# Batch 2's scores two steps earlier, its token cast ahead of batch 1's exponentials, and the states of batches 2 and 3 fetched sooner

## The chip, the cores and the metric

The kernel runs on one core of one Trainium2 chip. A core has five engines with a queue of instructions each: TensorE (PE in the profile; its weight loads are PEld), VectorE (DVE), ScalarE (ACT), GpSimd (POOL) and SyncE (SP), which here only issues DMAs. Each engine runs its queue in order and waits at an instruction until the semaphores that it names have been raised. The metric is the device time of one execution in microseconds; a time is the median of several runs.

## The reference

Eight batches of 512 tokens and 32 states, eight heads of 64 numbers each, go through a cross attention in both directions, and what comes out goes through a feed-forward layer with a leaky ReLU:

```
scores  = scale * x @ state^T          # tokens look at states
a       = softmax(scores);   xread = a @ state
scores2 = scale * state @ x^T          # states look at tokens
a2      = softmax(scores2);  sread = a2 @ x
x       = concat([xread, sread])       # 4352 rows of 512
out     = leaky_relu(x @ w_in, 0.01) @ w_out      # w_in 512x2048, w_out 2048x512
```

## The kernel before, in words

The product xread @ w_in is never made from xread. For each batch the states are multiplied with w_in first (`a_m`, line 339: the result M has 256 rows, one for each head and state, and 2048 columns, made in four column chunks of 512), and the hidden layer is then M^T times the softmax weights aT (`ff1`, line 369: two matmuls of 128x512 for each of 16 steps, and a ScalarE Prelu out of PSUM, line 377; `ff1_pair`, line 379, does two steps into one bank pair). `piece` (line 481) is four matmuls of the second layer for a block of 128 tokens; after the last of its four quarters the block is copied out of PSUM (`y_store`, line 494) and stored by a DMA from SP.

A batch goes through these stages before its `ff1`:

- `load_x` (line 97): the tokens come as fp32 into `xl`, of which there is one buffer, so that the next batch's load waits for the casts out of it. Batch 2's load is issued on GpSimd's queue early on, behind the loads of the weights and of batch 1's tokens (`x1`).
- `cast_x` (line 104): tokens to bf16, in halves on ScalarE and GpSimd for batch 2 and on GpSimd alone later.
- `a_xt_dma` (line 189): a transposing DMA from SP makes `xT`.
- `load_state` (line 166) fetches the states of two batches (first group: 2 and 3) with eight small DMAs from SP, after a VectorE memset of the same tile; `state_t` (line 175) casts them on GpSimd and transposes them by a DMA from SP (`st_t`).
- `a_scores` (line 202): eight matmuls into the PSUM tile `sc`. There is one such tile for all batches.
- `a_shift`, `a_exp`, `a_probs`: the softmax over states (VectorE, one ScalarE exponential at line 233, VectorE), which gives aT. `a_max2`, `a_exp2` (two exponentials straight out of `sc`, line 274), `a_probs2`: the softmax over tokens, which gives a2, and `a_a2t`, its transposing DMA from SP.

The order of all instructions is written by hand: each engine runs its own in the order in which the program's text issues them. PSUM is shared by tags: "ph" and "py" have two banks each and "big" and "sc" are one pair of banks each. So `a_m(a2, 0, "big")` and the wide `ff1_pair` of steps 6 and 10, also "big", must take turns, and an eviction (`m_evict`, line 359) ends each turn.

The stretch that the change touches begins at line 835, where batch 0's hidden layer is done and batch 1's tokens are cast (VectorE, line 836). Batch 0's second layer fills TensorE while batch 1 is prepared: its tokens are transposed on TensorE (line 853), then come its scores, its M and its softmax. Lines 869 to 888 hold batch 1's second exponentials, the states' and tokens' preparation of batch 2 and the load of batch 3. The loop at line 895 then does the 16 steps of batch 1's hidden layer. After each odd step a `piece` is slipped in (two last ones of batch 0, then six of batch 1), after step 5 batch 2's scores and its first chunk of M, at step 7 the transposing DMA of batch 3's tokens, and at steps 9, 11 and 13 batch 2's exponentials. Lines 916 to 921 close the stretch: both batches' `a_probs2`, batch 1's `a_a2t`, and two more chunks of M. From line 927 on, batches 2 to 7 run through a steady loop whose second layer is done by a scheme with fewer multiplications (line 557).

Of the kernel before, what the change touches and what calls it, by code (L numbers as in the profile page):

```python
# [10 lines left out]
B, H, S, D = 8, 8, 512, 64  # L11
# [16 lines left out]
def kernel(  # L28
# [9 lines left out]
    nc = tc.nc  # L38
# [15 lines left out]
    VEC, SCA, POO = nc.vector.tensor_copy, nc.scalar.copy, nc.gpsimd.tensor_copy  # L54
# [49 lines left out]
    def cast_x(b, h0, h1, copy):  # L104
        copy(  # L105
            xs[b][:, :, h0:h1].rearrange("p t h d -> p h t d"),
            xl[b][:, h0:h1].rearrange("p h (t d) -> p h t d", t=NT),
        )
# [54 lines left out]
    stf = [consts.tile([P, hi - lo, P], FP32, name=f"stf{lo}", tag=f"stf{lo}") for lo, hi in groups]  # L163
    stb = [consts.tile([P, hi - lo, P], BF16, name=f"stb{lo}") for lo, hi in groups]

    def load_state(i):
        lo, hi = groups[i]
        for k in range(NK):
            for g in range(2):
                nc.sync.dma_start(  # L170
                    stf[i][NS * k:NS * (k + 1), :, D * g:D * (g + 1)],
                    state[lo:hi, 2 * k + g].rearrange("b n d -> n b d"),
                )
# [10 lines left out]
    def a_open(a, b):  # L184
        a.b = b
        a.xb = xs[b]
        a.xT = att.tile([P, NT, NK, P], BF16, name="xT", tag="xT")
# [43 lines left out]
    def block_exp(sh, n):  # L231
        e1 = att.tile([P, n * NS], BF16, name="e1", tag="e1", bufs=1)
        nc.scalar.activation(out=e1[:], in_=sh[:], func=AF.Exp, scale=SCALE)
        return e1

    def block_probs(dst, e1, n):
        r1 = att.tile([P, n], FP32, name="r1", tag="r1")
        nc.vector.tensor_reduce(
            out=r1[:], in_=e1[:].rearrange("p (c j) -> p c j", j=NS),
            axis=AX.X, op=ALU.add, apply_transpose=True,  # L240
        )
        nc.vector.tensor_scalar(out=r1[:], in0=r1[:], scalar1=1e-9, scalar2=None, op0=ALU.add)
        q1h = att.tile([P, n], BF16, name="qh", tag="qh")
        with nc.allow_low_precision(reason="one rounding, of the finished reciprocal"):
            nc.vector.reciprocal(q1h[:], r1[:])
        q1b = att.tile([P, n, NS], BF16, name="qb", tag="qb", bufs=1)
        nc.vector.transpose(q1b[:], q1h[:, :, None].to_broadcast([P, n, NS]))
        nc.vector.tensor_tensor(
            out=dst, in0=e1[:].rearrange("p (g s) -> p g s", g=2),
            in1=q1b[:].rearrange("p (g c) j -> p g (c j)", g=2), op=ALU.mult,  # L250
        )
# [5 lines left out]
    def a_exp(a):  # L257
        a.e1 = block_exp(a.sh, NB)

    def a_probs(a):  # L260
        a.aT = att.tile([P, 2, S], BF16, name="aT", tag="aT")
        block_probs(a.aT[:], a.e1, NB)

    def a_max2(a):
        m2 = att.tile([P, 2], FP32, name="mcol", tag="mcol")
        nc.vector.tensor_reduce(out=m2[:], in_=a.sc[:], axis=AX.X, op=ALU.max, negate=True)  # L266
        a.m2s = att.tile([P, 2], FP32, name="mcols", tag="mcols")
        nc.vector.tensor_scalar(out=a.m2s[:], in0=m2[:], scalar1=SCALE, scalar2=None, op0=ALU.mult)

    def a_exp2(a, g):  # L270
        if g == 0:
            a.e2 = att.tile([P, 2, S], BF16, name="e2", tag="e2")
            a.r2 = att.tile([P, 2], FP32, name="r2", tag="r2")
        nc.scalar.activation(  # L274
            out=a.e2[:, g], in_=a.sc[:, g, :], func=AF.Exp,
            bias=a.m2s[:, g:g + 1], scale=SCALE, accum_out=a.r2[:, g:g + 1],
        )

    def a_probs2(a):
        nc.vector.tensor_scalar(out=a.r2[:], in0=a.r2[:], scalar1=1e-9, scalar2=None, op0=ALU.add)  # L280
        q2 = att.tile([P, 2], FP32, name="qc", tag="qc")
        nc.vector.reciprocal(q2[:], a.r2[:])
        a.a2 = att.tile([P, 2, S], BF16, name="a2", tag="a2")
        for g in range(2):
            nc.vector.tensor_scalar(
                out=a.a2[:, g, :], in0=a.e2[:, g, :],
                scalar1=q2[:, g:g + 1], scalar2=None, op0=ALU.mult,
            )

    def a_a2t(a):  # L290
        a.a2T = att.tile([P, 2, NT, P], BF16, name="a2T", tag="a2T")
        nc.sync.dma_start_transpose(
            a.a2T[:].rearrange("p g i q -> p (g i) q"), a.a2[:].rearrange("p g s -> p (g s)")
        )
# [64 lines left out]
    def m_evict(a, c, pm, copy):  # L359
        cols = slice(DM * c, DM * (c + 1))  # L360
        if isinstance(pm, list):
            for g in range(2):
                copy(a.M[:, g, cols], pm[g][:])
        else:
            copy(a.M[:, :, cols], pm[:])  # L365
# [115 lines left out]
    def piece(b, hT, i, jq, bank=None, copy=SCA):  # L481
        if jq == 0:
            y = ys[b, i] = Y()
            y.py = psum.tile([P, DM], FP32, name="py", tag="py")[:] if bank is None else bank
        y = ys[b, i]
        for j in range(4 * jq, 4 * jq + 4):
            nc.tensor.matmul(  # L487
                y.py, lhsT=hT[:, j, P * i:P * (i + 1)], rhs=w_out_bf[:, j, :],
                start=(j == 0), stop=(j == 15),
            )  # L490
        if jq == 3 and copy is not None:
            y_store(b, i, copy)

    def y_store(b, i, copy):
        tag, bufs = (f"yo{i - 2}", 1) if (b, i) in ((0, 2), (0, 3)) else ("ysb", 3)
        ysb = ypool.tile([P, DM], FP32, name="ysb", tag=tag, bufs=bufs)
        copy(ysb[:], ys[b, i].py)
        if b == B:
            for bb in range(4):
                r0 = (4 * i + bb) * SROW + S  # L500
                nc.sync.dma_start(out[r0:r0 + NS, :], ysb[NS * bb:NS * (bb + 1), :])
        else:
            nc.sync.dma_start(rows_of(b)[i], ysb[:])
# [140 lines left out]
    a0, a1, a2 = att_of[:3]  # L644
# [149 lines left out]
    def open_ff1_0(tag):  # L794
        if tag == "sc":
            pr = psum.tile([P, 2, S], FP32, name="php", tag=tag, bufs=1)
            return pr, [pr[:, 0], pr[:, 1]]
        ph = [psum.tile([P, S], FP32, name="ph", tag=tag) for _ in range(2)]
        return ph, [p[:] for p in ph]

    def ff1_0(banks, j, g, vs=(0, 1)):
        for v in vs:
            nc.tensor.matmul(  # L803
                banks[v], lhsT=a0.M[:, g, P * (j + v):P * (j + v + 1)], rhs=a0.aT[:, g, :],
                start=(g == 0), stop=(g == 1),
            )
# [19 lines left out]
    for j, tag in ((4, "py"), (6, "sc"), (8, "py"), (10, "ph"), (12, "py"), (14, "ph")):  # L826
        t, bk = open_ff1_0(tag)
        for g in range(2):
            ff1_0(bk, j, g)
        relu0(t, j)  # L830
        if j == 8:
            m_evict(a0, 3, a_m(a0, 3, "big"), VEC)
            a_scores(a0)
            a_max2(a0)
    for u in range(2):
        VEC(
            a1.xb[:, :, NK * u:NK * (u + 1)].rearrange("p t h d -> p h t d"),
            x1[u][:].rearrange("p h (t d) -> p h t d", t=NT),
        )
    nc.vector.memset(stf[0][:, 0, D - 1:D + 1], 0.0)  # L840
    load_state(0)

    for g in range(2):
        a_exp2(a0, g)
# [21 lines left out]
    for i in (2, 3):  # L866
        piece(0, h0, i, 1)
    m_evict(a1, 3, a_m(a1, 3, "ph"), SCA)
    for g in range(2):
        a_exp2(a1, g)  # L870
    open_xb(2)
    state_t(0)
    cast_x(2, 0, 4, SCA)
    cast_x(2, 4, 8, POO)
    a_open(a2, 2)
    a_xt_dma(a2)
# [17 lines left out]
    fill = [(0, h0, 0, 3), (0, h0, 1, 3)] + [(1, h1, i, jq) for jq in range(3) for i in range(2)]  # L894
    for s in range(16):
        if s in (6, 10):
            ff1_pair(a1, h1, s, "big")
        elif s not in (7, 11):
            ff1(a1, h1, s)
        if s == 5:  # L900
            a_scores(a2)
            m_evict(a2, 0, a_m(a2, 0, "big"), SCA)
            a_shift(a2)
            a_max2(a2)
        if s % 2:
            pb, hT, i, jq = fill[s // 2]
            piece(pb, hT, i, jq, copy=VEC if s == 3 else SCA)
        if s == 7:
            a_open(att_of[3], 3)
            a_xt_dma(att_of[3])  # L910
        elif s == 9:
            a_exp(a2)
            a_probs(a2)
        elif s in (11, 13):
            a_exp2(a2, s // 2 - 5)
    a_probs2(a2)
    a_probs2(a1)
    a_a2t(a1)
    pm = [a_m(a2, 1, "big"), a_m(a2, 2, "sc")]
    m_evict(a2, 1, pm[0], VEC)  # L920
    m_evict(a2, 2, pm[1], SCA)

# [2 lines left out]
    for b in range(2, B):  # L927
        hT = hpool.tile([P, 16, S], BF16, name="hT", tag="hT")
# [15 lines left out]
        for s in range(16):  # L944
# [71 lines left out]
            if std:  # L1016
                i, jq = std.pop(0)
# [102 lines left out]
```

## Time and profile before

| what | us |
|---|---|
| median of 3 runs (lowest, highest) | 205.06 (204.99, 205.19) |
| the profiled execution | 204.74 |
| its span, from the first to the last instruction | 202.9 |
| TensorE busy in the span | 196.8 |
| VectorE, ScalarE, GpSimd busy | 152.7, 143.3, 42.3 |
| bytes moved, mean rate in the span | 27.99 MB, 138 GB/s |

The profile page is one execution as the hardware profiler recorded it. Its times count from the first instruction. It gives the busy time of each engine, the span in 40 slices with tenths of busy time, the DMA queues (q0: those issued on GpSimd's queue, q1: those of SP's, q8 and q14: instructions that the engines fetch), and the chain of work that ended last, followed back from the end. Besides the page the trace answers questions: the timeline of an engine gives start, length, engine, line, what is written from what, and in brackets how long the engine was idle before and what ended that; the DMA views give packets by queue in a stretch of time, and the time from a DMA's issue to its landing. The granted TensorE clock was 1.00 over the span. From some 28 us on until 193 us the slices of TensorE are all at nine tenths or more.

### The profile page before, as it was taken

How to read it: one execution, taken by the hardware profiler on the slowest of the kernel's cores; microseconds unless marked ns; L12 is line 12 of the kernel's file. 1: busy time of each engine (PE TensorE's matmuls, PEld its weight loads, DVE VectorE, ACT ScalarE, POOL GpSimd, SP SyncE). 2: the span in 40 equal slices, each digit the busy share in tenths (PEclk: the TensorE clock that was granted, in tenths of full speed). 3: DMA queues.
4: the chain of work that ended last, by engine and by line, in shares of the span. 5: the costliest groups of instructions: out<-in, count | busy, mean ns of one | idle time of the engine just before them, and what ended most of it. 6: DMA issues, size and time to landing. Idle time of an engine off the chain costs nothing.

```text
span 202.9 us, 4755 instructions
## 1 busy us (share of the span) xinstructions
PE 196.8 (97%) x1964; PEld 125.7 (62%) x1964; DVE 152.7 (75%) x231; ACT 143.3 (71%) x264; POOL 42.3 (21%) x66
## 2 busy tenths in 40 slices
PE   7989999999999999999999999999999999999993
PEld 2543534434344567766776767776767677799882
DVE  1767689689999969976997699769968853686612
ACT  3558748579869796978797878788778856467710
POOL 8931002022007004400251040200020002004250
PEclk9999999999999999999999999999999999999999
DMA  5999994799396986538946795250017000410035
GB/s 187 227 207 277 229 252 131 147 304 236 64 265 190 104 183 159 103 117 256 122 30 181 236 131 105 103 158 5 0 50 213 18 0 28 182 55 0 3 89 170
DMA packets 39733, 27.99 MB, mean 138 GB/s; under 512 B 25312, under 2 KB 36704, under 8 KB 39712
## 3 DMA queue, kind: packets, MB, share of 16 engines
q1 hardware_dynamic: 34512, 20.88, 42.9%
q0 software_dynamic: 4912, 6.55, 15.8%
q8 instruction: 15, 0.25, 0.5%
q10 hardware_dynamic: 288, 0.26, 0.5%
q14 instruction: 6, 0.05, 0.1%
HBM read 17.30 MB, written 8.91 MB: 129 GB/s over the span
## 4 chain that ended last, share of the span: by engine, by line
PE 89%; DMA 5%; POOL 2%; ACT 1%; DVE 1%; issue 0%; POOLq 0%
PE yq L557 36%; PE ph L372 23%; PE py L487 10%; DMA w_in_bf<-in_moe_w_in_dram 5%; PE pm L351 4%; PE pyw L487 3%; PE pf L441 3%; PE yu L557 3%; PE ph L803 2%; PE psn L318 1%; PE sc L206 1%; PE phw L383 1%; POOL w_in_bf L118 1%; DVE M L365 1%; ACT hT L377 1%; ACT M L365 1%
## 5 line engine op out<-in xcount | busy, mean ns | idle before, releaser
L377 ACT ACTIVATE hT<-ph 128x512 bf16<-128x512 f32 x108 | 63.6, 604 | 22.0 <-PE ph L372 21.5
L372 PE MATMUL ph<-aT,M 128*128 128x512 bf16 x216 | 62.3, 379 | 0.0
L557 PEld LDWEIGHTS <-su 128*128 128x128 bf16 x416 | 39.7, 98 | 14.5 <-DVE su L546 1.7
L557 PEld LDWEIGHTS <-hT 128*128 128x128 bf16 x288 | 27.7, 98 | 11.8 <-issue 1.1
L105 POOL CAST xb<-xl 128x512 bf16<-128x512 f32 (+1 forms) x21 | 16.4, 818 | 61.1 <-DMA xl<-in_x_dram 61.1
L557 PE MATMUL yq<-tw_xf,su 128*128 128x256 bf16 x192 | 27.2, 273 | 0.0
L557 PE MATMUL yq<-w_out_bf,hT 128*128 128x256 bf16 x192 | 27.0, 273 | 0.0
L372 PEld LDWEIGHTS <-M 128*128 128x128 bf16 x216 | 21.0, 98 | 9.1 <-DVE r L280 0.4
L546 DVE TENSOR_TENSOR su<-hT 128x1024 bf16<-128x1024 bf16 x24 | 16.9, 702 | 10.5 <-ACT hT L377 10.5
L487 PE MATMUL py<-w_out_bf,hT 128*128 128x512 bf16 x96 | 24.2, 380 | 0.0
L487 PEld LDWEIGHTS <-hT 128*128 128x128 bf16 x128 | 12.0, 98 | 14.8 <-issue 1.3
L627 POOL TENSOR_TENSOR yo<-sv,sv 128x512 f32<-128x512 f32 x6 | 7.8, 1300 | 52.8 <-ACT sv L566 41.3
L569 DVE TENSOR_TENSOR yo<-yq,sv 128x512 f32<-128x512 f32 x17 | 11.6, 685 | 6.5 <-PE yq L557 6.5
L566 ACT COPY sv<-yq 128x512 f32<-128x512 f32 x24 | 13.9, 585 | 2.0 <-PE yq L557 1.4
L365 ACT CAST M<-pm 128x1024 bf16<-128x1024 f32 x13 | 13.2, 1014 | 0.6 <-PE pm L351 0.6
L557 PE MATMUL yq<-w_out_bf,su 128*128 128x256 bf16 x96 | 13.1, 273 | 0.0
L557 PE MATMUL yq<-tw_x,su 128*128 128x256 bf16 x96 | 13.1, 273 | 0.0
L557 PE MATMUL yq<-tw_x,hT 128*128 128x256 bf16 x88 | 12.1, 273 | 0.0
L274 ACT ACTIVATE e<-sc,mcols 128x512 bf16<-128x512 f32 x16 | 11.1, 696 | 0.0
L216 DVE TRANSPOSE_TENSOR_REDUCE mrow<-sc 128x32 f32<-128x1024 f32 x7 | 8.7, 1243 | 1.4 <-PE sc L206 1.4
L266 DVE TENSOR_REDUCE mcol<-sc 128x2 f32<-128x1024 f32 x8 | 9.7, 1214 | 0.0
L224 DVE STREAM_TRANSPOSE mrowb<-mrow 128x1024 f32<-128x1024 f32 x7 | 8.7, 1245 | 0.2
(148 smaller groups left out, 271.5 us busy)
## 6 DMA issues: line engine op xcount, KB each, us to landing
xl<-in_x_dram SPq DMA_DIRECT2D x5, 1024.0 KB, 6.8
out_dram<-yo SPq DMA_DIRECT2D x10, 512.0 KB, 2.8
w_in_bf<-in_moe_w_in_dram POOLq DMA_DIRECT2D x4, 512.0 KB, 8.9
w_out_bf<-in_moe_w_out_dram POOLq DMA_DIRECT2D x4, 512.0 KB, 16.9
out_dram<-ysb SPq DMA_DIRECT2D x8, 256.0 KB, 5.4
xf<-in_x_dram SPq DMA_DIRECT2D x2, 512.0 KB, 4.8
x<-in_x_dram POOLq DMA_DIRECT2D x2, 512.0 KB, 14.0
xl<-in_x_dram POOLq DMA_DIRECT2D x1, 1024.0 KB, 19.1
```

Of the source, the lines that this page charges most:

```text
L105: copy(xs[b][:, :, h0:h1].rearrange("p t h d -> p h t d"), xl[b][:, h0:h1].rearrange("p h (t d) -> p h t d", t=NT),)
L216: nc.vector.tensor_reduce(out=m1[:], in_=flat.rearrange("p (c j) -> p c j", j=NS), axis=AX.X, op=ALU.max, apply_transpose=True,)
L266: nc.vector.tensor_reduce(out=m2[:], in_=a.sc[:], axis=AX.X, op=ALU.max, negate=True)
L274: nc.scalar.activation(out=a.e2[:, g], in_=a.sc[:, g, :], func=AF.Exp, bias=a.m2s[:, g:g + 1], scale=SCALE, accum_out=a.r2[:, g:g + 1],)
L365: copy(a.M[:, :, cols], pm[:])
L372: nc.tensor.matmul(ph[:], lhsT=a.M[:, g, P * j:P * (j + 1)], rhs=a.aT[:, g, :], start=(g == 0), stop=(g == 1),)
L377: nc.scalar.activation(out=hT[:, j, :], in_=ph[:], func=AF.Prelu, alpha=0.01)
L487: nc.tensor.matmul(y.py, lhsT=hT[:, j, P * i:P * (i + 1)], rhs=w_out_bf[:, j, :], start=(j == 0), stop=(j == 15),)
L546: (eng or nc.vector).tensor_tensor(out=S[n][:, ms], in0=u[:, ms], in1=v[:, ms], op=op)
L557: nc.tensor.matmul(bank[:, i, :], lhsT=lhs[:, m, P * i:P * (i + 1)], rhs=rhs[:, m, :], start=(first and m == 0 and (i == 0 or of is not No ...
L566: copy(t[:], bank)
L569: nc.vector.tensor_tensor(out=dst, in0=bank, in1=self.sv[n][:], op=ALU.add)
```

## The change

Four edits. In the preparation, the memset of the states' tile and the eight state DMAs go ahead of the two VectorE casts of batch 1's tokens. Batch 1's two second exponentials go behind the states' transpose and ScalarE's half of batch 2's token cast. In the loop over batch 1's steps, batch 2's scores, its first chunk of M with the eviction, and its maxima go from step 5, ahead of the piece, to step 3, behind the piece, whose copy out of PSUM goes from VectorE to ScalarE; batch 2's exponential and probabilities go from step 9 to step 7, its two second exponentials from steps 11 and 13 to 9 and 11. Behind the loop, batch 1's `a_probs2` and `a_a2t` go behind the two evictions of M. No instruction is added or removed but that one copy, which changes engines; SP's and GpSimd's own orders stay as they are.

```diff
             a_max2(a0)
+    nc.vector.memset(stf[0][:, 0, D - 1:D + 1], 0.0)
+    load_state(0)
     for u in range(2):
         VEC(
             a1.xb[:, :, NK * u:NK * (u + 1)].rearrange("p t h d -> p h t d"),
             x1[u][:].rearrange("p h (t d) -> p h t d", t=NT),
         )
-    nc.vector.memset(stf[0][:, 0, D - 1:D + 1], 0.0)
-    load_state(0)
...
     m_evict(a1, 3, a_m(a1, 3, "ph"), SCA)
-    for g in range(2):
-        a_exp2(a1, g)
     open_xb(2)
     state_t(0)
     cast_x(2, 0, 4, SCA)
+    for g in range(2):
+        a_exp2(a1, g)
     cast_x(2, 4, 8, POO)
...
             ff1(a1, h1, s)
-        if s == 5:
+        if s % 2:
+            pb, hT, i, jq = fill[s // 2]
+            piece(pb, hT, i, jq)
+        if s == 3:
             a_scores(a2)
             m_evict(a2, 0, a_m(a2, 0, "big"), SCA)
             a_shift(a2)
             a_max2(a2)
-        if s % 2:
-            pb, hT, i, jq = fill[s // 2]
-            piece(pb, hT, i, jq, copy=VEC if s == 3 else SCA)
         if s == 7:
+            a_exp(a2)
+            a_probs(a2)
             a_open(att_of[3], 3)
             a_xt_dma(att_of[3])
-        elif s == 9:
-            a_exp(a2)
-            a_probs(a2)
-        elif s in (11, 13):
-            a_exp2(a2, s // 2 - 5)
+        elif s in (9, 11):
+            a_exp2(a2, s // 2 - 4)
     a_probs2(a2)
-    a_probs2(a1)
-    a_a2t(a1)
     pm = [a_m(a2, 1, "big"), a_m(a2, 2, "sc")]
     m_evict(a2, 1, pm[0], VEC)
     m_evict(a2, 2, pm[1], SCA)
+    a_probs2(a1)
+    a_a2t(a1)
```

## The prediction

> **What bounds the kernel now.** I read the page first: its busy times, its slices and its chain.
>
> ```profile
> PE 196.8 (97%) x1964; PEld 125.7 (62%) x1964; DVE 152.7 (75%) x231; ACT 143.3 (71%) x264; POOL 42.3 (21%) x66
> PE   7989999999999999999999999999999999999993
> PE 89%; DMA 5%; POOL 2%; ACT 1%; DVE 1%; issue 0%; POOLq 0%
> ```
>
> TensorE is the bound from some 20 us to the end. A change can win only where TensorE really stands still, and "busy" hides short stands, since ends of matmuls are modelled. So I read starts. In the timeline of PE, 16 matmuls of 128x512 begin at 32.92 us and what follows them at 36.38 us: 0.216 us each, 0.86 us for four. These are the lines around the change (start us, length us, engine, line, what):
>
> ```profile
> 39.83 1.03 PE L372 MATMUL ph<-aT,M 128*128 128x512 bf16 x4
> 40.82 0.41 PE L206 MATMUL sc<-xT,st_t 64*32 64x512 bf16 x8
> 41.03 0.41 PE L351 MATMUL pm<-w_in_bf,st_t 64*32 64x512 bf16 x8
> 41.38 1.04 PE L487 MATMUL py<-w_out_bf,hT 128*128 128x512 bf16 x4
> 42.64 0.59 PE L383 MATMUL phw<-aT,M 128*128 128x512 bf16 x2 [0.22 <-ACT M L365]
> ```
>
> The scores (sc) were due at 39.83 + 0.86 = 40.69 and began at 40.82. Of these 0.13 us, 0.10 is what each turn to 64-row weights costs (the pm groups at 28.67 and 30.84 began 0.10 after they were due); so 0.03 is a wait, for xT, which landed at 40.78 (below). The pair (phw) was due at 41.38 + 0.86 = 42.24 and began at 42.64: **0.40 us lost**, for ScalarE's eviction of pm, which holds the bank "big" that the pair needs. From there to 66 us I find no further stand over 0.1 us. So between 30 and 66 us this kernel has 0.43 us to give back.
>
> Why the scores can't simply come earlier is told by the queues behind them. ScalarE:
>
> ```profile
> 33.16 0.70 ACT L274 ACTIVATE e<-sc,mcols 128x512 bf16<-128x512 f32 x1
> 33.73 0.22 ACT L274 ACTIVATION_READ_ACCUMULATOR e<-sc,mcols 128x1 f32 x1
> 34.43 1.05 ACT L105 CAST xb<-xl 128x1024 bf16<-128x1024 f32 x1 [0.48 <-DMA xl<-in_x_dram]
> ```
>
> GpSimd's half of the cast, and then SP's two transposes:
>
> ```profile
> 34.46 1.04 POOL L105 CAST xb<-xl 128x1024 bf16<-128x1024 f32 x1 [0.29 <-DMA xl<-in_x_dram]
> ```
>
> ```profile
> 34.20 1.26 SPq L177 DMA_TRANSPOSE st_t<-stb  x1
> 35.65 1.83 SPq L190 DMA_TRANSPOSE xT<-xb  x1
> ```
>
> Both halves begin when xl, the tokens of batch 2, has landed (34.41), not when their engines come free: ScalarE had been idle 0.48 us. SP issues xT 0.15 us after GpSimd's half ends (35.50). The same line over that window gives xT's flight:
>
> ```profile
> DMA to landing us min/median/max: 5.1/5.1/5.1
> ```
>
> 35.65 + 5.13 = 40.78. In the trace's semaphore record 15 of the 16 steps of that landing are in by 40.00; the last, at 40.78, is one DMA engine's, which at 39.42 took up a fetch of instructions (8 KB, 0.31 us, the q14 row of the DMA view of 39.4 to 39.5). Flights of the six xT transposes: 5.1, 4.4, 6.0, 4.2, 5.0, 4.4 us.
>
> **The change, part by part.** Times are on the profiled execution's clock; that run took 204.74 us (span 202.9), the median shown is 205.06. I work out a difference and add it to the median.
>
> *Scores and eviction two steps up.* Now they follow the piece of step 3, ahead of the matmuls of steps 4 and 5. They fall due where the x4 at 39.83 began, plus 0.10: 39.93. ScalarE evicts pm 0.68 after the scores begin at the earliest (pm ends at 0.62), so by 1.70 after; the pair is due 2.28 after (0.56 for scores and pm, 0.86 for steps 4 and 5, 0.86 for the piece). The 0.40 goes: **-0.40**. What is late next is xT itself: the scores wait until 0.04 after it lands (as 40.78 to 40.82), so TensorE stands for xT + 0.04 - 39.93. If xT lands at 40.78 again, that is 0.89 against the 0.03 that goes: a loss of 0.46. It breaks even at xT = 40.32, and the whole 0.43 is won at 39.89 or earlier.
>
> *Token cast ahead of batch 1's two exponentials (L274).* In the trace the cast waits for xl, so this moves nothing: **0**. It puts the exponentials behind the cast: 35.48 + 1.46 (32.49 to 33.95) = 36.94, and ScalarE's next work, the relu of step 0, is released at 37.01. Covered by 0.07; if xl is late by 0.3, that relu is late by 0.23, and TensorE first needs its bank at 38.10, 0.49 after the relu's end of 37.61. The scores' bank sc is read by them until 36.94, long before 39.93.
>
> *States fetched ahead.* The memset and the eight DMAs go from 23.97 to about 21.45 (right behind mcols at 21.22 to 21.39, where VectorE is idle 0.42 us). SP has nothing else there. What they pass is the second half of batch 1's tokens (landing at 23.20; TensorE needs it, cast, at 24.88, slack 0.97) and w_out's second quarter (25.59, needed at 26.84, slack 1.25). The states' 640 packets took 18 to 31 ns, 18 us over 16 engines: 1.1 us an engine at most. The DMA views show none of their packets before 27.4, 3.5 us after the first issue, so the first half of that slack is not touched. **0**, at worst 0.2. The states land 2.5 us sooner, about 31.0 for 33.49, and their cast on GpSimd moves from 33.77 to about 31.3 (beside VectorE work from PSUM; the cast at 33.77 left the transpose of VectorE at its 1.25), SP's st_t from 34.20 to 31.7. That frees SP before xT: issue at 35.53 for 35.65, **-0.12** on xT. But st_t's 288 packets, which ran at 35.4 to 36.2 on idle engines, now run from about 33.0 (1.25 after issue, as before), beside the end of xl, whose last engine moves 4 KB packets until 33.93, one each 0.18 us. On that engine st_t has 18 packets of 18 to 38 ns (its own time; the stretch of a 4 KB packet from 182 to 220 beside others): **+0 to +0.6 on xl**, and so on both casts and xT. I take 0.15, by the row of the unmixed packets, half of which fit in.
>
> [...]
>
> *xT's flight.* Issue then is at 35.53 + 0.15, say 35.65 again; flights run from 4.2 to 6.0. [...] I take 4.9, between the median 4.7 and this row's 5.1: xT at 40.55, a stand of 0.66 less the 0.03 that goes: **+0.63**.
>
> *The rest.* The copy of the piece of step 3 goes from VectorE (0.69) to ScalarE (0.58), which was idle 0.58 there: 0; uncovered, it would hold the eviction by 0.58, which 2.28 - 1.70 = 0.58 still hides. Batch 2's exponential (L233) is ready 4.3 after the scores (VectorE 41.30 to 45.09 before) and runs ahead of the relus of steps 8 and 9, the two L274 around the pair of step 10. Adding ScalarE's starts: relus at 5.26 and 5.74, L274 at 6.22, pair 6.88, L274 7.80, relu of 12 at 8.46 to 9.06. TensorE needs that bank at 9.18: covered by 0.1, about 0.1 lost if not. The softmax of batch 1's second side goes behind the eviction of M: 1.22 + 0.93 us of VectorE change places, so a2T of batch 1 is issued about 0.7 later (52.79), and behind it on SP xl of batch 4 (54.08), a2T, two stores and the second states (58.84). Their users wait elsewhere: a2T's sread is at 67.07 (landed 56.09), batch 4's tokens and states are first used at 88: **0**.
>
> Sum: -0.40 + 0.63 = **+0.23 us: 205.3**. The change is then undone by its own wait: TensorE stands before the scores and no longer before the pair.
>
> **Rivals.** *xT in time.* If st_t stays clear of xl and xT flies 4.2 to 4.4, it lands at 39.8 to 39.95: -0.43 to -0.37, **204.65**. For it: 15 of 16 engines took 4.35 even here, and 0.12 less on SP may bring the last packets past the fetch. Against it: the median of the six flights, and this very one, are longer. [...]
>
> *Slower: st_t in xl's tail.* With +0.3 to +0.6 on xl, SP issues xT at 35.83 to 36.13, and a flight of 5.1 ends at 40.93 to 41.23: a stand of 1.04 to 1.34, net +0.6 to +0.9, **205.8**; a flight of 6.0 would make it +1.8. It decides as slower from xT at about 40.75 (+0.43). For it: that engine is the last of xl's, with no slack. Against: most engines are idle by 33, and st_t may arrive late.
>
> *It doesn't do what it says.* xl may arrive sooner or later for causes of its own, since all of this hangs on it; the cast is moved up in the text and not in time. That is in the forecast.
>
> **How the numbers follow.** Forecast (xT at 40.3 to 40.95: -0.0 to +0.6, own range 205.0 to 205.65): 0.44. xT in time, 39.8 to 40.3 (204.6 to 205.05): 0.30. st_t in xl's tail: 0.22. A late token half early on or a lost bank, slower: 0.04. A measurement here can tell about 0.2%, 0.41 us. Faster by more needs xT at 39.91 or sooner: 0.21 of the second case. Slower by more takes 0.13 of the first and the last two but 0.01: 0.38. The same: 0.41. The range leaves out the deep end of the slow cases: 204.6 to 206.2.
>
> **What would show it.** Right: phw of step 6 begins with no stand; sc begins 0.04 after xT lands, near 40.6; xl's cast at 34.4 to 34.7; the cadence from 55 us on unchanged and shifted by the sum. Wrong: cast before 34.3 or xT's flight under 4.5 (first rival); cast after 34.8 (second); any stand between 55 and 190 us that was not there, or transposes (pxt) later than 24.88, which no case holds.

## The result and the profile after

| | before | changed |
|---|---|---|
| median of 22 runs (lowest, highest), us | 204.96 (204.48, 205.39) | 205.87 (204.59, 206.70) |
| profiled execution, its span | 204.74, 202.9 | 205.86, 204.1 |

The ratio is 1.0045, 95% interval 1.0035 to 1.0055: slower by some 0.9 us, inside the stated range, over the forecast's own 205.0 to 205.65 and where the second rival put it. Of the page's chain of work 17% are transfers now, 5% before:

```profile
PE 78%; DMA 17%; POOL 2%; issue 0%; DVE 0%; POOLq 0%
```

This is that chain from 33 us on, in order of time (start us, length us, what):

```profile
15.46 20.03 DMA xl<-in_x_dram
35.49 0.05 issue
35.54 1.35 POOL xb L105
36.89 0.02 issue
36.91 4.59 DMA xT<-xb
41.50 0.04 issue
41.55 0.41 PE sc L206 x8
```

The path to the scores is a row without a gap: batch 2's tokens land at 35.49 (34.41 before), GpSimd's half of the cast takes 1.34 (1.04 before), xT flies 4.59. TensorE waits at the end of it, and no longer at the pair, as its timeline shows:

```profile
39.36 1.02 PE L487 MATMUL py<-w_out_bf,hT 128*128 128x512 bf16 x4
41.55 0.41 PE L206 MATMUL sc<-xT,st_t 64*32 64x512 bf16 x8 [1.16 <-DMA xT<-xb]
41.76 0.41 PE L351 MATMUL pm<-w_in_bf,st_t 64*32 64x512 bf16 x8
42.10 1.04 PE L372 MATMUL ph<-aT,M 128*128 128x512 bf16 x4
42.98 1.03 PE L487 MATMUL py<-w_out_bf,hT 128*128 128x512 bf16 x4
43.84 1.03 PE L383 MATMUL phw<-aT,M 128*128 128x512 bf16 x4
```

The pair (phw) follows its piece by 0.86, the pace of four matmuls: its stand is gone. The begin of a run shifts all these times (batch 1's scores start at 26.13 to 27.00 in the traces), so I compare traces by the distances between the starts of successive batches' scores: batch 1 to 2, 2 to 3, 3 to 4. Batch 4 to 5 is 21.05 in every trace, and so is what follows (107.0).

| trace | 1 to 2 | 2 to 3 | 3 to 4 | sum against before | time against before | ratio, 95% interval |
|---|---|---|---|---|---|---|
| before | 14.54 | 12.93 | 21.17 | | | |
| changed | 14.92 | 13.44 | 21.08 | +0.80 | +0.91 | 1.0035 to 1.0055 |
| after_again | 14.57 | 13.44 | 22.05 | +1.42 | +0.78 | 1.0026 to 1.0054 |
| states_back | 14.51 | 13.43 | 21.98 | +1.28 | +0.94 | 1.0030 to 1.0055 |
| states_only | 14.67 | 12.93 | 21.17 | +0.13 | +0.01 | 0.9993 to 1.0010 |
| transpose_gated | 15.01 | 13.44 | 21.81 | +1.62 | +1.41 | 1.0061 to 1.0110 |
| a2t_back | 14.63 | 13.44 | 21.08 | +0.51 | +0.72 | 1.0022 to 1.0050 |
| a2t_only | 14.51 | 12.93 | 21.60 | +0.40 | +0.37 | 1.0001 to 1.0026 |
| scores_only | 14.46 | 13.44 | 21.08 | +0.34 | +0.60 | 1.0016 to 1.0040 |
| scores_at_4 | 14.67 | 13.44 | 21.08 | +0.55 | +0.49 | 1.0012 to 1.0031 |
| pair_later | 14.50 | 12.69 | 21.41 | -0.04 | -0.04 | 0.9983 to 1.0010 |
| cast_only | 14.50 | 12.93 | 21.19 | -0.02 | -0.12 | 0.9987 to 1.0009 |
| tokens_sooner | 13.64 | 13.44 | 21.18 | -0.38 | -0.25 | 0.9981 to 1.0010 |
| tokens_sooner_2 | 13.64 | 13.45 | 21.18 | -0.37 | -0.15 | 0.9977 to 1.0003 |

With the scores at step 3 the first distance is 13.64 when nothing waits (tokens_sooner); what is above it is the stand before batch 2's scores. The sum is one trace's, and leaves out what comes ahead of batch 1's scores; the time is a median.

### The profile page after: what moved, and what is told of

Read it like the earlier page. It is cut to its first block, busy times and chain, and to the rows that moved or that the text cites. A ratio compares the mean times of both kernels' runs of the same rounds, so it can differ in the third digit from the quotient of the medians.

```text
span 204.1 us, 4755 instructions
## 1 busy us (share of the span) xinstructions
PE 197.3 (97%) x1964; PEld 126.1 (62%) x1964; DVE 151.8 (74%) x230; ACT 143.7 (70%) x265; POOL 41.5 (20%) x66
## 4 chain that ended last, share of the span: by engine, by line
PE 78%; DMA 17%; POOL 2%; issue 0%; DVE 0%; POOLq 0%
PE yq L557 36%; PE ph L372 22%; DMA xl<-in_x_dram 10%; PE py L487 7%; DMA w_in_bf<-in_moe_w_in_dram 5%; PE pm L351 3%; PE pf L441 3%; PE yu L557 3%; DMA xT<-xb 2%; PE psn L318 1%; PE sc L206 1%; PE phw L383 1%; POOL w_in_bf L118 1%; POOL xb L105 1%; PE yz L557 0%
## 5 line engine op out<-in xcount | busy, mean ns | idle before, releaser
L105 POOL CAST xb<-xl 128x512 bf16<-128x512 f32 (+1 forms) x21 | 15.8, 790 | 64.0 <-DMA xl<-in_x_dram 64.0
L247 DVE STREAM_TRANSPOSE qb<-qh 128x1024 bf16<-128x1024 bf16 x7 | 8.7, 1245 | 0.2
```

The source lines that it names most:

```text
L105: copy(xs[b][:, :, h0:h1].rearrange("p t h d -> p h t d"), xl[b][:, h0:h1].rearrange("p h (t d) -> p h t d", t=NT),)
```

## The experiments: which edit costs

Theory A, at first: the states' transpose st_t, now issued while batch 2's tokens still move, holds back their landing. B: the states' early packets do. C: the late landing was chance. In the changed kernel SP issues st_t at 31.92 (34.20 before), and xl's packets run until 34.17:

```profile
31.92 1.26 SPq L177 DMA_TRANSPOSE st_t<-stb  x1
36.91 2.86 SPq L190 DMA_TRANSPOSE xT<-xb  x1
```

**after_again** is the changed kernel itself, for a second trace.

> The changed kernel once more, for a second trace of it. Theory A (held landing): the states' transpose st_t is issued at about 32, while xl is still moving, and xl's landing is raised only when st_t's packets are written too: xl lands at 35.2 to 35.6, 1 us or more after its own last data packet, and sc begins at 41.2 to 41.8 after a stand of about 1 us; time 0.6 to 1.2 us over the kernel before. Theory B (the states' eight early DMAs push xl back by their packets): xl lands as late, but 0.5 us after its last data packet, which itself comes at 34.8 or later. Theory C (chance of the one trace: xl lands late in any kernel now and then, and the early scores merely show it): xl lands at 34.3 to 34.7 in this trace and the time is within 0.3 us of before.

The tokens landed at 35.14, 1.27 after their last packet (A, not B), and the scores stood 14.57 - 13.64 = 0.93. But a second stand appeared that nobody had foretold, before the scores of batch 4:

```profile
76.53 0.41 PE L206 MATMUL sc<-xT,st_t 64*32 64x512 bf16 x8 [0.90 <-DMA xT<-xb]
```

**states_back** puts the state loads back.

```diff
-    nc.vector.memset(stf[0][:, 0, D - 1:D + 1], 0.0)
-    load_state(0)
     for u in range(2):
         VEC(
...
         )
+    nc.vector.memset(stf[0][:, 0, D - 1:D + 1], 0.0)
+    load_state(0)
```

> The changed kernel with the memset and the eight state DMAs back behind the casts of batch 1's tokens; scores at step 3 and all else stay. A and B: st_t is issued at about 34.3, after xl has landed at 34.3 to 34.6, xT lands at 40.0 to 40.8, sc begins at 40.05 to 40.85 (due at 39.93), the pair of step 6 has no stand: from 0.3 us under before to 0.5 us over it. C: no different from the changed kernel, 0.6 to 1.2 us over before.

The tokens landed in time (34.15) and xT within A's range (40.69), but the time was C's: 0.94 over. The early states are not what costs most. Batch 4's scores stood here too (21.98).

**states_only** is the kernel before with the opposite diff and nothing else.

> The kernel before with nothing but the memset and the state DMAs moved ahead of the casts of batch 1's tokens; scores stay at step 5, due at 40.79. A and B: xl lands at 35.2 to 35.6, xT at 41.2 to 41.7, so sc begins 0.4 to 0.9 us late and the pair's 0.40 stays lost: 0.4 to 0.9 us over before. C: xl at 34.4, the time within 0.2 us of before.

The time was C's, within 0.1% of before; ScalarE's half of the cast began at 34.72, xT landed at 41.01, and the scores came 0.13 later than before. A's hold is in this trace all the same. A landing is counted in 16 steps: before, they came in one by one from 32.20 to 34.41; here all 16 came between 34.59 and 34.70, behind st_t's last data packet (34.38). Since xl's own last packet came only at 34.16, the hold cost the whole landing next to nothing.

**transpose_gated** holds st_t back until the tokens are in.

```diff
     open_xb(2)
+    gate = consts.tile([P, 1], FP32, name="gate")
+    POO(gate[:], xl[2][:, 0, 0:1])
     state_t(0)
```

> The changed kernel, states fetched early, but GpSimd first copies one element per partition of xl into a spare tile, so that the cast of the states and with it st_t come only after xl has landed. A: xl lands at 34.3 to 34.7; st_t is issued at about 35.0, the GpSimd half of the token cast ends at about 36.0, xT is issued at 36.1 to 36.4 (behind st_t's 1.26 us on SP) and lands at 40.5 to 41.3; sc begins earlier than in the changed kernel by 0.2 to 1.0 us. B: xl lands at 35.2 to 35.6 all the same, and everything behind it comes 0.5 us later than in the changed kernel. C: xl anywhere.

The tokens landed at 34.01, 0.53 after their last packet: A against B. But in series behind the gate xT was issued at 36.31, the scores came no sooner (15.01, a miss), and batch 4 stood too: the slowest kernel of all. A holds for the landing and explains little of the time.

So theory D: two stands, the second made by the last edit. SP issues a2T of batch 1, batch 4's tokens, the second states (L170), their st_t and batch 4's xT in that order, each behind the other. These are SP's lines of the kernel before, then of after_again:

```profile
52.79 1.23 SPq L292 DMA_TRANSPOSE a2T<-a  x1
54.08 0.57 SPq L99 DMA_DIRECT2D xl<-in_x_dram  x1
...
58.84 4.94 SPq L170 DMA_DIRECT2D stf<-in_state_dram  x8
...
66.24 1.19 SPq L177 DMA_TRANSPOSE st_t<-stb  x1
...
68.11 3.97 SPq L190 DMA_TRANSPOSE xT<-xb  x1
```

```profile
54.76 1.23 SPq L292 DMA_TRANSPOSE a2T<-a  x1
56.05 1.47 SPq L99 DMA_DIRECT2D xl<-in_x_dram  x1
...
61.33 5.84 SPq L170 DMA_DIRECT2D stf<-in_state_dram  x8
...
69.54 1.77 SPq L177 DMA_TRANSPOSE st_t<-stb  x1
...
71.99 2.21 SPq L190 DMA_TRANSPOSE xT<-xb  x1
```

Before, that xT landed at 74.08 and the scores used it at 74.92: 0.84 to spare. In after_again it landed at 76.49.

**a2t_back** (the changed kernel) and **a2t_only** (the kernel before) take the last edit away and make it alone.

```diff
     a_probs2(a2)
+    a_probs2(a1)
+    a_a2t(a1)
     pm = [a_m(a2, 1, "big"), a_m(a2, 2, "sc")]
     m_evict(a2, 1, pm[0], VEC)
     m_evict(a2, 2, pm[1], SCA)
-    a_probs2(a1)
-    a_a2t(a1)
```

> The changed kernel with its last edit undone: batch 1's second softmax and its transpose a2T go ahead of the two evictions of M again. Theory D (two stands): the change loses time at two places, before batch 2's scores (0.9 to 1.2 us of stand, against the 0.40 before the pair that it wins) and before batch 4's scores, because SP issues a2T of batch 1, batch 4's tokens and the second states behind it about 1.2 us later. Then here the stand before batch 4's scores (0.0 and 1.0 us in the two traces of the changed kernel) is gone, xT of batch 4 lands 1 us or more before it is due, and the time is 0.3 to 0.7 us over before. Theory C' (only the first stand counts, batch 4's is chance): as the changed kernel, 0.7 to 1.0 us over before.

> The kernel before with the last edit alone. D: xT of batch 4, which landed 0.84 us before it was used, lands 1.2 to 2.3 us later, so that batch 4's scores stand 0.3 to 1.2 us and the time is 0.3 to 1.0 us over before. C': within 0.2 us of before.

Both as D said, in the trace: the third distance is 21.08 without the edit and 21.60 with it alone. There xT landed at 75.84, and the scores waited for it:

```profile
75.88 0.41 PE L206 MATMUL sc<-xT,st_t 64*32 64x512 bf16 x8 [0.39 <-DMA xT<-xb]
```

In time the two tell less. a2t_only costs 0.37, its interval (0.02 to 0.53) just clear of none. a2t_back is 0.72 over (0.45 to 1.02): that is in the range of C' and just above D's, so by time alone taking the edit out of the changed kernel shows no gain.

**scores_only** makes the loop's edit alone, **scores_at_4** the same with one line more:

```diff
-        if s == 3:
+        if s == 4:
             a_scores(a2)
```

> The kernel before with the edit of the loop alone (scores and eviction after the piece of step 3, exponentials two steps up); states, token cast and a2T as before. D: xl lands at 34.2 to 34.5, xT at 40.6 to 40.9 with one DMA engine 0.8 us behind the others where the instruction fetch falls into its end; the scores stand 0.6 to 0.9, the pair's 0.40 is won: 0.2 to 0.5 us over before, and no stand before batch 4's scores. C': the same.

> As the run before, but batch 2's scores and eviction follow step 4 instead of step 3, so that they are due 0.43 us later, at about 40.4, and the eviction still ends before the pair of step 6 is due. D: the scores stand 0.2 to 0.5, the pair's 0.40 is won: from 0.2 us under before to 0.1 over it. C': the same.

scores_only: xT landed at 41.42, one of its 16 steps 0.83 behind the others; the stand is 0.82, and +0.34 stays after the pair's gain: D. Its time is 0.60 over, above D's range of 0.2 to 0.5, though its interval (0.33 to 0.82) reaches into it. scores_at_4 missed its range (0.49 over): xT came no earlier, and at step 14 TensorE lost 0.41 (due at 48.88 + 0.86 = 49.74) to a bank that a ScalarE relu frees, which stood behind batch 2's second exponential:

```profile
50.15 1.08 PE L372 MATMUL ph<-aT,M 128*128 128x512 bf16 x4 [0.25 <-ACT hT L377]
```

**cast_only** makes the second edit alone; **pair_later**, a new edit on the kernel before, moves the piece of step 7 ahead of the pair of steps 6 and 7.

```diff
-        if s % 2:
-            pb, hT, i, jq = fill[s // 2]
+        for n in {5: (2, 3), 7: ()}.get(s, (s // 2,) if s % 2 else ()):
+            pb, hT, i, jq = fill[n]
             piece(pb, hT, i, jq, copy=VEC if s == 3 else SCA)
```

> The kernel before with batch 1's two exponentials behind the states' transpose and ScalarE's half of the token cast, and nothing else. D: the cast still waits for xl, the relu of step 0 begins at most 0.1 us late: within 0.15 us of before. Rival: the exponentials hold up the relus of steps 0 and 1 and with them a bank that step 2 needs, 0.1 to 0.3 us over before.

> The kernel before with one edit of its own: the piece of step 7 moves ahead of the pair of steps 6 and 7, so that ScalarE's eviction of batch 2's M ends before the pair is due. Scores stay at step 5. Theory D (the 0.40 before the pair is the only true stand of the kernel before, and it can be had without asking for the scores sooner): no stand at the pair, none elsewhere, from 0.3 to 0.45 us under before. Rival (ScalarE's relus of the pair and of steps 8 and 9 now come in one row and hold a bank): the 0.4 comes back at step 12 or 14, within 0.1 us of before.

cast_only costs nothing that the runs can tell. pair_later wins 0.24 in the second distance and loses 0.24 in the third, where batch 3's first matmuls for M (pm) begin 0.32 late, 0.05 after VectorE's eviction of M ends (54.29): no change.

**tokens_sooner** tests the core of it: is the scores' price at step 3 nothing but xT's landing? Batch 2's tokens are loaded ahead of the last quarter of w_out, and xT is issued ahead of st_t.

```diff
-    for c in range(1, 4):
+    for c in range(1, 3):
         load_w_out(c)
     load_x(2, nc.gpsimd)
+    load_w_out(3)
...
     open_xb(2)
-    state_t(0)
     cast_x(2, 0, 4, SCA)
...
     a_xt_dma(a2)
+    state_t(0)
```

(on the changed kernel, with the early states and the last edit undone)

> The changed kernel with its last edit and the early states undone, with batch 2's tokens loaded ahead of the last quarter of w_out on GpSimd's queue, and with the token cast and xT ahead of the states' cast and transpose. Scores at step 3. D (the scores' price at step 3 is nothing but xT's landing): xl lands 2.5 to 3.1 us sooner, xT is issued at 33.5 to 34.0 and lands at 37.8 to 39.0, st_t at 38 to 38.6, before the scores are due at 39.93; neither scores nor pair stand: 0.3 to 0.5 us under before, if the last quarter of w_out, due at 34.65, lands by then (expected 34.4; each 0.1 us later costs as much). Rival (the early scores crowd ScalarE's queue and hold banks of steps 12 to 15 whenever they come): a stand of 0.1 to 0.4 at step 14 remains, the time within 0.2 us of before.

> The same kernel as tokens_sooner, timed a second time, since its first interval (0.9981 to 1.001) holds both no change and the 0.38 us that its trace shows from batch 1's scores to batch 5's. D: between 0.2 and 0.45 us under before, interval below 1. Rival (what the trace wins is lost in other executions, where w_out's last quarter or xT comes later): within 0.15 us of before.

xT landed at 39.61, st_t at 39.89, later than expected but in time, and neither scores nor pair stand:

```profile
39.06 1.03 PE L487 MATMUL py<-w_out_bf,hT 128*128 128x512 bf16 x4
40.02 0.41 PE L206 MATMUL sc<-xT,st_t 64*32 64x512 bf16 x8
```

Two traces win 0.38 and 0.37, within what was expected. The medians are 0.25 and 0.15 under before, both short of their ranges, and both intervals hold 1: whether this kernel is faster than before is not settled. That the 0.60 of scores_only is gone is shown: its interval ends at 1.0010 at most, and that of scores_only begins at 1.0016.

## Why the prediction was right or wrong

- **What TensorE could win: right.** The 0.40 before the pair is won wherever the eviction comes earlier, the due time 39.93 - 26.28 = 13.65 after batch 1's scores is tokens_sooner's 13.64, and the scores began 0.05 after xT landed in the changed kernel.
- **Moving the cast: right**, no gain and no price beyond the noise (cast_only).
- **The stand of 0.66 before the scores: mis-sized.** It was 14.92 - 13.64 = 1.28 in the first trace of the changed kernel. Measured from batch 1's scores, the tokens landed 0.74 later than before, where I had taken 0.15; GpSimd's cast took 0.30 more, where I had nothing; xT's flight was 4.59, where I had 4.9. The next three points take these terms in turn.
- **"+0 to +0.6 on xl ... I take 0.15":** the mechanism was the second rival's, st_t in xl's tail, but not by packets that share an engine: xl's last 4 KB packets took 0.18 as before, and its last packet of all (4 bytes) came at 34.17, which is 0.10 sooner than before if measured from batch 1's scores. The landing came 1.32 after that (0.48 before), so this step alone is 0.84 longer. In eight traces where st_t is issued after xl's last packet, that step is 0.48 to 0.53. Where it is issued ahead, it is 1.32, 1.27, 1.09 and 0.54, and the landing comes 0.3 to 0.5 after st_t's own last data packet (35.03, 34.68, 34.24, 34.38). The gate, which puts st_t behind the landing, takes the hold away (0.53). By what means st_t's packets hold the landing is not shown: the traces' packets don't name the engine.
- **xT's issue:** I had 1.04 for GpSimd's cast. It took 1.34 and 1.54, because it now began while VectorE's aT product ran (below). This is the term that I had not seen at all.
- **xT's flight, 4.9:** 4.59 and 4.25 in the changed kernel, 5.2 to 5.3 in states_back, scores_only and a2t_back, where one step came late beside a fetch of instructions (below). I take this to be why states_back and the changed kernel differ so little in the first distance: the earlier tokens of states_back met the fetch. In the changed kernel the fetch came at 38.49 and 37.92, 2.5 us and more ahead of xT's last data packet. The 4.9 was my estimate, with the fetch expected where it was; what sets the fetch's time no run shows.
- **"Batch 4's tokens and states are first used at 88": wrong.** Its scores start at 74.92, in batch 3's loop, 0.84 after xT's landing. I had read one batch too far. Pushing a2T back on SP made a second stand: 0.37 us alone (a2t_only), and 0 or 0.97 in the changed kernel's two traces. It is also a sign that I had named as one that no case holds, a new stand between 55 and 190 us.

Alone, the four edits measure +0.01 (states), -0.12 (cast), +0.60 (scores; 0.33 to 0.82) and +0.37 (a2T; 0.02 to 0.53): together 0.86, against 0.91 and 0.78. So the change is slow for two of its edits, scores that ask for xT sooner than it comes and a transpose pushed back at the head of SP's queue; their shares are known no better than these intervals. That the median came out at the second rival's 205.8 is partly luck: that rival had no place for the slower cast, the shorter flight or batch 4's stand.

What stays open is why medians and single traces differ by up to 0.6 us. The landings scatter from run to run (xT's flight was 4.59 and 4.25 in the changed kernel's two traces), and a trace is one draw: the changed kernel's 22 runs lie 2.1 us apart and those of the kernel before 0.9, as they would if TensorE now waits for such landings, but no run here separates that.

## What to carry to other kernels

Before a consumer is moved up, follow its operand to the last landing and see what that waits for: here the whole gain was 0.43 us and the operand came 0.8 to 1.4 late in every kernel that asked at step 3 without loading it sooner. Before anything is moved back, go down the DMA queue behind it to each first use, by start times in the trace and not by loop counts. A transposing DMA beside the end of a load can hold that load's landing after its data is in: here to 1.1 to 1.3 us after the last packet in three traces, for 0.5 without.

## What the runs showed of the hardware

GpSimd's cast (1.04 alone) and VectorE's bf16 product aT (0.69 alone) hardly run beside each other. In the nine traces where they met, whichever began first kept its time, and the other ended 0.14 to 0.15 us sooner than if it had begun only then. The kernel before and the changed kernel, GpSimd then VectorE each:

```profile
34.46 1.04 POOL L105 CAST xb<-xl 128x1024 bf16<-128x1024 f32 x1 [0.29 <-DMA xl<-in_x_dram]
34.95 1.09 DVE L248 TENSOR_TENSOR aT<-e,qb 128x1024 bf16<-128x1024 bf16 x1
```

```profile
35.54 1.34 POOL L105 CAST xb<-xl 128x1024 bf16<-128x1024 f32 x1 [3.65 <-DMA xl<-in_x_dram]
35.29 0.69 DVE L248 TENSOR_TENSOR aT<-e,qb 128x1024 bf16<-128x1024 bf16 x1
```

What keeps the two apart the traces don't show; these lengths are all that they give.

In eight traces a fetch of 8 KB of instructions (0.31 us) began within 0.06 us of the end of xT's last data packet. In seven of them one of the 16 steps of xT's landing came 0.78 to 0.87 us behind the others (40.00 and 40.78 before, 39.82 and 40.69 in states_back, 40.59 and 41.42 in scores_only), in cast_only 0.26. In the changed kernel, whose fetch came at 38.49, all 16 were in within 0.2 us. That the fetch delays that step, and that both are one DMA engine's, as the prediction has it, is read from the times alone: no record names the engine, and the delay is longer than the fetch.
